# Pooled attention with a top-k MoE layer: long loads and stores, chunk order, dense layers cut into sixteen pieces

## The chip, the cores and the metric

One core of a Trainium2 chip runs the kernel in one launch. The metric is the device time of the launch in microseconds, the median of the runs. TensorE (PE, with its weight loads PEld), VectorE (DVE), ScalarE (ACT), GpSimd (POOL) and SyncE (SP, which here only issues DMAs) each run their own list of instructions in order and wait for one another by semaphores.

## The reference, cut to what matters

```python
# q, k, v: (8 batches, 8 heads, 576 tokens, 64) float32
k_p, v_p = mean over 8 neighbouring tokens        # 72 pooled tokens a head
attn = softmax(q @ k_p.T / 8);  x = attn @ v_p    # -> x: (8, 576, 512)
scores = x @ w_gate                               # one number a token
out = x.copy()
for b in range(8):                                # the 128 best tokens of each batch
    top = argpartition(-scores[b], 128)[:128]
    ye  = relu(x[b, top] @ w1) @ w2               # 512 -> 1024 -> 512
    out[b, top] += sigmoid(scores[b, top])[:, None] * ye
```

## The kernel before, in words

All the work is in `direct_path`; `general_path` runs only if a softmax sum is out of range, which it isn't here. Scheduling is by hand: the order in which the Python code calls its functions is the order on each engine.

A batch has 576 tokens, taken as six **chunks** of 96 (`C`); two chunks are a **unit** (`u`, 24 of them). For each batch the kernel loads K, Q and V, sums K and V over groups of eight tokens (`pool_k`, `pool_v`, three or four GpSimd additions each, L184 to L202), transposes K and Q by DVE (`k_trans` L191, `q_trans` L212), multiplies them (`scores`, L222) and takes the exponential on ACT (L227). `attend` (L237) multiplies a chunk's exponentials with the value sums; two more columns of these give the softmax sum and the gate score. `norm` (L249 to L254, all DVE) reads that result from PSUM, divides, and puts the chunk in `xs`. The PSUM tile `pA` of `attend` has one buffer, so the next `attend` waits for `norm`.

Then follows the MoE layer of the batch, while later batches attend: `store_x` writes `xs` to the output, `score` sums the gate scores, `row_bcast` spreads them over partitions, `count` (L315 to L319, six of them) ranks each token, `one_hot` and `gather` find the 128 best rows and fetch them from the output by an indirect DMA that GpSimd issues (L341), `x_trans` (L353) transposes them on TensorE, `hidden` (L369) and `finish` (L380) are the two dense layers, and a second indirect DMA (L386) writes the rows back.

The main loop goes over units and has five slots in each. A table, `jobs`, filled by `at(u, slot, ...)`, says in which slot of which unit a step of the MoE layer stands. `hidden` and `finish` stand there in four pieces each, for one batch all within two units of the three of a batch. All loads and stores are issued by SP, in the order of the code; a load waits there until its buffer is free. K goes in by four DMAs of 24 or 32 partitions, a Q of a batch by three of 128 partitions, V by two halves of 64 and 8 partitions; `store_x` writes six DMAs of 16 partitions.

Of the kernel before, what the change touches and what calls it, by code (L numbers as in the profile page):

```python
# [830 lines left out]
```

## Time and profile before

| | us |
|---|---|
| median of three runs | 385.44 (384.58 to 387.45) |
| profiled execution, its own time | 386.28 |
| its span, first to last instruction | 384.7 |
| PE busy | 289.5 (75%) |
| PEld busy | 226.8 (59%) |
| DVE busy | 173.1 (45%) |
| POOL busy | 153.4 (40%) |
| ACT busy | 57.4 (15%) |

The profile is of one execution. "Busy" is time in which an engine executed something; matmuls are pipelined and their ends modelled, so PE's busy time is not work at full speed. The granted clock is the share of TensorE's 2.4 GHz that the chip allowed: 1.0 is 2.4 GHz, 0.5 is 1.2 GHz. Times in the trace are counted from the start of the span.

### The profile page before, as it was taken

What the parts mean: (1) busy time and instruction counts of PE and PEld (TensorE: products, weight loads), DVE (VectorE), ACT (ScalarE), POOL (GpSimd) and SP (SyncE); (2) the same over time, 40 slices, a digit from 0 to 9 for tenths busy, and PEclk for the clock granted to TensorE, in tenths of its full rate; (3) what the DMA queues carried; (4) which work ended last, traced back from release to release, by engine and by line L of the source; (5) the groups of instructions that cost most, each with busy time, mean ns of one, the idle gap of its engine ahead of it and who ended that gap; (6) DMA issues with size and microseconds to landing.
All of it is one profiled execution on the core that took longest, in us unless ns stands there. A gap on an engine that the chain in (4) does not pass through costs nothing.

```text
span 384.7 us, 5966 instructions
## 1 busy us (share of the span) xinstructions
PE 289.5 (75%) x2306; PEld 226.8 (59%) x2306; DVE 173.1 (45%) x664; ACT 57.4 (15%) x73; POOL 153.4 (40%) x165
## 2 busy tenths in 40 slices
PE   0228888534999589959996899768994999896890
PEld 0127776432885378539863787457853985782750
DVE  2503535924366433924392528452574338346000
ACT  1001112100221112101220122021210131010100
POOL 0277911465612782068506670478017500202001
PEclk9999856555999688975998599967997699789697
DMA  8999999989798469715993389436000420160001
GB/s 179 254 187 231 347 200 156 180 177 200 157 173 158 95 137 170 145 27 118 196 160 77 89 178 179 104 89 125 2 0 27 103 51 0 56 123 28 29 0 37
DMA packets 18041, 47.55 MB, mean 124 GB/s; under 512 B 2252, under 2 KB 2252, under 8 KB 17172
## 3 DMA queue, kind: packets, MB, share of 16 engines
q1 hardware_dynamic: 16724, 42.88, 55.1%
q0 software_dynamic: 1280, 4.20, 3.5%
q8 instruction: 20, 0.33, 0.4%
q14 instruction: 17, 0.14, 0.1%
HBM read 35.54 MB, written 11.53 MB: 122 GB/s over the span
## 4 chain that ended last, share of the span: by engine, by line
DMA 30%; issue 20%; POOL 19%; PE 14%; SPq 11%; DVE 4%; ACT 0%; POOLq 0%; ACTq 0%
DMA vraw<-in_v_dram 11%; DMA kraw<-in_k_dram 7%; DMA qraw<-in_q_dram 7%; SPq L100 5%; PE pM L369 5%; POOL vraw L198 5%; DMA xr<-out_dram,idx 5%; SPq L275 4%; PE pF L380 3%; POOL kraw L184 3%; POOL vraw L199 3%; PE pA L237 3%; PE pS L222 2%; POOL vp L200 2%; POOL vraw L202 1%
## 5 line engine op out<-in xcount | busy, mean ns | idle before, releaser
L237 PEld LDWEIGHTS pA<-vp,et 72*96 72x96 f32 x768 | 86.4, 195 | 31.8 <-issue 25.4
L237 PE MATMUL pA<-vp,et 72*96 72x66 f32 x768 | 89.8, 280 | 18.4 <-DVE vp L203 10.2
L222 PE MATMUL pS<-qt,kt 32*72 32x192 f32 x768 | 55.1, 445 | 31.6 <-DVE zin L293 15.8
L369 PE MATMUL pM<-xg,w 128*128 128x128 f32 x512 | 75.3, 311 | 1.4 <-ACT xg L355 0.7
L369 PEld LDWEIGHTS pM<-xg,w 128*128 128x128 f32 x512 | 70.8, 222 | 4.2 <-issue 2.1
L222 PEld LDWEIGHTS pS<-qt,kt 32*72 32x72 f32 x768 | 37.9, 192 | 45.6 <-DVE zin L293 17.7
L380 PE MATMUL pF<-w,ht 128*128 128x512 f32 x128 | 61.2, 607 | 0.0
L227 ACT ACTIVATE et<-pS 72x1536 f32<-72x1536 f32 x24 | 34.7, 1446 | 116.9 <-PE pS L222 116.9
L337 POOL TENSOR_SCALAR idx<-tok 128x1 int32<-128x1 f32 x8 | 2.0, 245 | 124.9 <-DVE g L339 124.9
L249 DVE TENSOR_SCALAR zall<-pA 96x8 f32<-96x8 f32 x48 | 7.4, 155 | 94.0 <-PE pA L237 94.0
L198 POOL TENSOR_TENSOR vraw<-vraw 72x1024 f32<-72x1024 f32 x16 | 37.7, 2356 | 16.9 <-DMA vraw<-in_v_dram 16.8
L252 DVE TENSOR_TENSOR xs<-pA,rz 96x512 f32<-96x512 f32 x48 | 32.9, 686 | 2.1
L380 PEld LDWEIGHTS pF<-w,ht 128*128 128x128 f32 x128 | 22.3, 191 | 19.3 <-issue 19.3
L317 DVE TENSOR_SCALAR_CACHE_REDUCE cmp<-sr,sc 96x576 bf16<-96x576 f32 (+5 forms) x48 | 26.6, 554 | 6.1 <-ACT sr L305 6.1
L184 POOL TENSOR_TENSOR kraw<-kraw 128x1536 f32<-128x1536 f32 x7 | 24.0, 3430 | 12.0 <-DMA kraw<-in_k_dram 12.0
L203 DVE TENSOR_REDUCE vp<-vraw 72x4 f32<-72x256 f32 x16 | 6.6, 416 | 46.8 <-POOL vraw L202 46.8
L353 PE MATMUL pM<-ident,xr 128*128 128x128 f32 x32 | 7.6, 381 | 23.5 <-DMA xr<-out_dram,idx 23.5
L212 DVE STREAM_TRANSPOSE qt<-qraw 128x768 f32<-128x768 f32 x24 | 23.0, 963 | 0.0
L386 POOL DMA_INDIRECT out_dram<-y,idx x8 | 8.5, 1064 | 35.2 <-DVE seen L471 20.1
L372 ACT ACTIVATE ht<-pM 128x512 f32<-128x512 f32 x16 | 9.6, 597 | 86.6 <-PE pM L369 86.6
L315 DVE TENSOR_SCALAR_CACHE_REDUCE cmp<-sr,sc 96x96 bf16<-96x96 f32 (+4 forms) x40 | 20.3, 506 | 1.2
L199 POOL TENSOR_TENSOR vraw<-vraw 72x512 f32<-72x512 f32 x16 | 20.3, 1266 | 1.3
(63 smaller groups left out, 194.3 us busy)
## 6 DMA issues: line engine op xcount, KB each, us to landing
qraw<-in_q_dram SPq DMA_DIRECT2D x24, 384.0 KB
out_dram<-xs SPq DMA_DIRECT2D x48, 192.0 KB
vraw<-in_v_dram SPq DMA_DIRECT2D x16, 512.0 KB
kraw<-in_k_dram SPq DMA_DIRECT2D x24, 288.0 KB
w<-in_moe_w_dram SPq DMA_DIRECT2D x2, 2048.0 KB
kraw<-in_k_dram SPq DMA_DIRECT2D x8, 384.0 KB
vraw<-in_v_dram SPq DMA_DIRECT2D x16, 64.0 KB
wg<-in_moe_w_gate_dram SPq DMA_DIRECT2D x1, 144.0 KB
```

Source lines behind the costliest of these rows:

```text
L184: eng.tensor_tensor(out=x[:, :, 0:4, :], in0=x[:, :, 0:4, :], in1=x[:, :, 4:8, :], op=OP.add)
L198: eng.tensor_tensor(out=x[:, :, 0:4, :], in0=x[:, :, 0:4, :], in1=x[:, :, 4:8, :], op=OP.add)
L199: eng.tensor_tensor(out=x[:, :, 0:2, :], in0=x[:, :, 0:2, :], in1=x[:, :, 2:4, :], op=OP.add)
L212: nc.vector.transpose(out=QT[u].rearrange("p j t c -> p t j c"), in_=QR[u].rearrange("p t (j e) -> p t j e", j=2))
L222: nc.tensor.matmul(p[:, i, N3 * s : N3 * s + N3], KT[b][r, j, KG * s : KG * s + KG, :].rearrange("p g r -> p (g r)"), QT[u][r, j, :, G * s ...
L227: nc.scalar.activation(ET[u].rearrange("p (i s) n -> p i (s n)", s=2), p[:, :, 0 : 2 * N3], AF.Exp, scale=exp_scale)
L237: nc.tensor.matmul(p[:, g, E * a : E * a + E], ET[u][:, h, C * cc : C * cc + C], VP[b][:, h, :], start=True, stop=True)
L252: nc.vector.tensor_tensor(out=XS[b][:, c, :].rearrange("p (g a d) -> p g a d", g=2, d=D), in0=o[:, :, :, 0:D], in1=rz.to_broadcast([C, 2, ...
L315: nc.vector.tensor_scalar(cmp[:, 0 : c * C], row[:, 0 : c * C], s, None, op0=OP.is_ge, op1=OP.add, accum_out=CN[b][:, c, 0:1])
L317: nc.vector.tensor_scalar(cmp[:, c * C : S], row[:, c * C : S], s, None, op0=OP.is_gt, op1=OP.add, accum_out=CN[b][:, c, 1:2])
L369: nc.tensor.matmul(p[:, NQ * (f4 % 2) + f, :], w1[:, d, 128 * fc : 128 * fc + 128], XG[b][:, d, :], start=(d == 0), stop=(d == DB - 1))
L380: nc.tensor.matmul(p, HT[b][:, f, :], w2[:, f, :], start=(f == 0), stop=(f == FB - 1))
```

## The change

Loads: K and Q of a batch are one DMA each over 128 partitions, 9 KB to a partition; the first V and the gate weights are issued by ACT. A partition of K now holds four and a half groups of tokens, so GpSimd sums quads only, DVE transposes the half sums (128 x 576 instead of 128 x 384) and adds them in pairs. Tokens are dealt to chunks otherwise (token 6p + c is row p of chunk c), so that a unit's store is one DMA of 96 partitions with 4 KB runs, issued by ACT; ACT writes the exponentials in permuted order for it. In `norm` ACT does the addition to the softmax sum and copies the gate column; the gate product is taken once a batch. `one_hot` is one DVE instruction instead of six. The range check of the sums is done once, at the end.

Order: the loop goes over chunks (`a`, 48 of them). `hidden` and `finish` are cut into eight pieces each and dealt over six chunks, two or three in a chunk. GpSimd's K sums, V sums and the gather have places of their own, and `k_trans` no longer stands behind a V sum. `row_bcast` uses the PSUM tile `pM` instead of `pF`.

```diff
     def load_k(b):
-        x = KRAW[b % 2].rearrange("p r t d -> p (r t d)")
-        run = KR * POOLW * D
-        for i in range(4):
-            n = 32 if b < 2 else 2 * KG
-            nc.sync.dma_start(
-                out=x[32 * i : 32 * i + n, :],
-                in_=bass.AP(tensor=k.tensor, offset=k.offset + (b * H + 2 * i) * S * D, ap=[[run, n], [1, run]]),
-            )
+        KR[b] = work.tile([128, TG, D], FT, name="kraw")
+        nc.sync.dma_start(out=KR[b], in_=k[b].rearrange("h (g t) d -> (h g) t d", g=G))
...
     def pool_k(b, eng):
-        x = KRAW[b % 2]
-        KS[b] = work.tile([128, KR, D], FT, name="ks", bufs=1)
-        eng.tensor_tensor(out=x[:, :, 0:4, :], in0=x[:, :, 0:4, :], in1=x[:, :, 4:8, :], op=OP.add)
+        x = KR[b].rearrange("p (r t) d -> p r t d", r=R)
+        KS[b] = work.tile([128, R, D], FT, name="ks", bufs=1)
         eng.tensor_tensor(out=x[:, :, 0:2, :], in0=x[:, :, 0:2, :], in1=x[:, :, 2:4, :], op=OP.add)
         eng.tensor_tensor(out=KS[b], in0=x[:, :, 0, :], in1=x[:, :, 1, :], op=OP.add)
...
+        nc.vector.tensor_tensor(out=KT[b].rearrange("p j s n -> p (j s n)"), in0=x[:, :, 0], in1=x[:, :, 1],
+                                op=OP.add)
...
-        nc.vector.tensor_scalar(z, o[:, :, :, D], 1e-9 * POOLW, None, op0=OP.add)
...
+        nc.scalar.activation(z.rearrange("p (g n) -> p g n", g=2), o[:, :, :, D], AF.Identity, bias=eps)
+        nc.scalar.copy(out=SS[b][:, c, :].rearrange("p (g n) -> p g n", g=2), in_=o[:, :, :, D + 1])
...
-    def store_x(b):
-        dst = out[b].rearrange("(g c t) d -> t g c d", g=G, c=NC)
-        store[b] = []
-        for t in range(CT):
-            i = nc.sync.dma_start(out=dst[t], in_=XS[b][G * t : G * t + G, :, :])
...
+    def store_x(u):
+        b, th = divmod(u, NTH)
+        c = slice(2 * th, 2 * th + 2)
+        i = nc.scalar.dma_start(out=out[b].rearrange("(p c) d -> p c d", c=NC)[:, c, :], in_=XS[b][:, c, :])
...
+    for u in range(NU):
+        at(2 * u + 2, 1, store_x, u)
     for b in range(B):
...
+        e = NC * (b + 1)
+        last = b == B - 1
+        at(e - 1, 3, score, b)
+        at(e, 2, row_bcast, b, 0)
+        at(e, 3, row_bcast, b, 1)
+        for c in range(NC):
+            at(e + (1 if last else (2, 2, 3, 3, 4, 5)[c]), 3, count, b, c)
+        at(e + (2 if last else 5), 3, one_hot, b)
+        at(e + (5 if last else 6), 3 if last else 1, gather, b)
+        at(e + 7, 1, gate, b)
+        at(e + 7, 3, x_trans, b)
+        for n, f in enumerate((0, 1, 2, 3, 4, 5, 8, 6, 7, 9, 10, 11, 12, 13, 14, 15)):
+            c = (0, 0, 1, 1, 2, 2, 2, 3, 3, 3, 4, 4, 4, 5, 5, 5)[n]
+            slot = (1, 2, 1, 2, 1, 2, 2, 1, 2, 2, 1, 2, 2, 1, 2, 2)[n]
+            at(e + 8 + c, slot, *((hidden, b, f) if f < 8 else (finish, b, f - 8)))
+        if b + 1 < B:
+            a = NC * b
+            at(a, 0, pool_k, b + 1, nc.gpsimd)
+            at(a + 1, 3, pool_v, b + 1, 0, nc.gpsimd)
+            at(a + 2, 1, k_trans, b + 1)
+            at(a + 3, 3, pool_v, b + 1, 1, nc.gpsimd)
+            at(a + 4, 3, gate_v, b + 1, 0)
+            at(a + 5, 3, gate_v, b + 1, 1)
```

What this moves on GpSimd, one batch's turn in the middle of the program. Before, from the K sums (L184 to L186) over the gather (L337 its indices, L341 the DMA) to the first V sums and the scatter (L386):

```order
L184 TENSOR_TENSOR kraw_70<-kraw_70 128x6x256
L185 TENSOR_TENSOR kraw_70<-kraw_70 128x6x128
L186 TENSOR_TENSOR ks<-kraw_70 128x384
L337 TENSOR_SCALAR idx<-tok 128x1
L341 DMA xr<-out_dram,idx 128x512
L346 TENSOR_SCALAR g<-g 128x1
L198 TENSOR_TENSOR vraw<-vraw 72x4x256
L199 TENSOR_TENSOR vraw<-vraw 72x4x128
L200 TENSOR_TENSOR vp_121<-vraw 72x4x64
L202 TENSOR_TENSOR vraw<-vp_121,wg 72x4x64
L386 DMA out_dram<-y,idx 4608x512
```

Now, the same turn:

```order
L169 TENSOR_TENSOR kraw<-kraw 128x9x128
L170 TENSOR_TENSOR ks<-kraw 128x576
L327 TENSOR_SCALAR idx<-tok 128x1
L331 DMA xr<-out_dram,idx 128x512
L340 TENSOR_SCALAR g<-g 128x1
L374 DMA out_dram<-y,idx 4608x512
L186 TENSOR_TENSOR vraw<-vraw 72x4x256
L187 TENSOR_TENSOR vraw<-vraw 72x4x128
L188 TENSOR_TENSOR vp_92<-vraw 72x4x64
L190 TENSOR_TENSOR vraw<-vp_92,wg 72x4x64
```

Both pairs of V sums now follow the scatter, and K's sums are two instructions instead of three. On DVE, before, the stretch from the one-hot rows to the next batch's transposed K (L191); L203 sums the gate column of V, L293 and L294 are the range check:

```order
L327 TENSOR_SCALAR oh<-slots,rank 96x128 x6
L335 TENSOR_REDUCE tok<-pM 128x1
L339 TENSOR_REDUCE g<-pM 128x1
L347 RECIPROCAL g<-g 128x1
L203 TENSOR_REDUCE vp_123<-vraw 72x4
L191 STREAM_TRANSPOSE kt<-ks 128x6x64
```

Now K is transposed (L175) and added in pairs (L179) two chunks into a batch, ahead of two counts (L301 to L309), and the V column (L194) comes later. The rows are from the first batches, where the steps of the batch before stand beside them:

```order
L247 RECIPROCAL rz<-zall 96x8
L248 TENSOR_TENSOR xs<-pA,rz 96x512
L175 STREAM_TRANSPOSE kh<-ks 128x9x64
L179 TENSOR_TENSOR kt<-kh 128x288
L204 STREAM_TRANSPOSE qt<-qraw 128x6x4x32
L301 MEMSET cn 96x1
L307 TENSOR_SCALAR cmp,cn<-sr,sc 96x576
L309 SCALAR_TENSOR_TENSOR cmp,cn<-sr,sc,before 96x96
L305 TENSOR_SCALAR cmp,cn<-sr,sc 96x96
```

The V column no longer stands between a batch's gather and its K. On TensorE, before, from the last piece of a batch's second layer (L380) to the next batch's dense work:

```order
L380 MATMUL pF<-w_131,ht 128x512 x2
L237 MATMUL pA<-vp_121,et 96x66 x8
L353 MATMUL pM<-ident,xr 128x128 x4
L222 MATMUL pS<-qt,kt 72x192 x16
L237 MATMUL pA<-vp_121,et 96x66 x8
L369 MATMUL pM<-xg,w_130 128x128 x8
L237 MATMUL pA<-vp_123,et 96x66 x8
L369 MATMUL pM<-xg,w_130 128x128 x8
```

Now (L216 scores, L368 second layer, L293 `row_bcast`, L232 `attend`, L346 transposed rows, L358 first layer):

```order
L216 MATMUL pS<-qt,kt 72x2x96 x16
L368 MATMUL pF<-w_104,ht 128x512 x2
L293 MATMUL pM<-ident,sc 96x96 x6
L232 MATMUL pA<-vp_94,et 96x66 x8
L368 MATMUL pF<-w_104,ht 128x512 x3
L346 MATMUL pM<-ident,xr 128x128 x4
L232 MATMUL pA<-vp_94,et 96x66 x8
L358 MATMUL pM<-xg,w_103 128x128 x4
L216 MATMUL pS<-qt,kt 72x2x96 x16
L358 MATMUL pM<-xg,w_103 128x128 x4
L232 MATMUL pA<-vp_94,et 96x66 x8
L358 MATMUL pM<-xg,w_103 128x128 x8
```

Between the gather's product and the transposed rows there are now a score group, `row_bcast`, an attend and five pieces of the second layer; before there was one piece and one attend.

## Rows read from the trace of the kernel before

**Rows 1.** Three stretches: busy us (instructions) by engine, granted clock, DMA share, GB/s.

```profile
0.00:95.90 95.90, 50.33 (x416) 41.14 (x416) 41.63 (x131) 11.54 (x11) 45.89 (x46) 0.75 0.97 211
95.90:334.40 238.50, 203.46 (x1717) 159.42 (x1714) 119.28 (x476) 41.99 (x54) 102.90 (x109) 0.86 0.53 106
334.40:384.70 50.30, 35.76 (x179) 26.19 (x178) 12.16 (x57) 3.85 (x8) 4.62 (x10) 0.84 0.18 41
```

**Rows 2.** Waits of PE in 95.9 to 334.4: total us, times, longest.

```profile
PE pS L222 <- DVE zin L293: 15.8, 5, 3.6
PE pM L353 <- DMA xr<-out_dram,idx: 10.3, 6, 2.2
```

**Rows 3.** Timeline, 206 to 216 us: start, length, engine, line, group [idle before, releaser].

```profile
206.59 2.36 POOL L198 TENSOR_TENSOR vraw<-vraw 72x1024 f32<-72x1024 f32 x1
211.87 0.42 DVE L203 TENSOR_REDUCE vp<-vraw 72x4 f32<-72x256 f32 x1 [5.02 <-POOL vraw L202]
212.21 0.84 DVE L191 STREAM_TRANSPOSE kt<-ks 128x384 f32<-128x384 f32 x1
213.11 2.85 PE L222 MATMUL pS<-qt,kt 32*72 32x192 f32 x32 [3.12 <-DVE zin L293]
215.88 2.83 PE L237 MATMUL pA<-vp,et 72*96 72x66 f32 x16
```

**Rows 4.** The two stretches around it: granted clock third from last.

```profile
182.00:206.00 24.00, 22.76 (x205) 16.92 (x203) 14.56 (x62) 4.97 (x7) 7.21 (x6) 1.00 0.88 166
213.00:222.00 9.00, 8.89 (x64) 7.98 (x65) 4.51 (x16) 1.45 (x1) 6.70 (x8) 0.50 0.47 105
```

**Rows 5.** Timeline, PE at the higher clock.

```profile
186.23 1.54 PE L222 MATMUL pS<-qt,kt 32*72 32x192 f32 x32
190.91 2.00 PE L369 MATMUL pM<-xg,w 128*128 128x128 f32 x16
192.75 1.50 PE L237 MATMUL pA<-vp,et 72*96 72x66 f32 x16
200.57 1.93 PE L380 MATMUL pF<-w,ht 128*128 128x512 f32 x4
```

**Rows 6.** Timeline, PE in the first batches.

```profile
22.93 1.52 PE L237 MATMUL pA<-vp,et 72*96 72x66 f32 x8 [4.29 <-DVE vp L203]
29.50 2.85 PE L222 MATMUL pS<-qt,kt 32*72 32x192 f32 x32
39.21 2.70 PE L222 MATMUL pS<-qt,kt 32*72 32x192 f32 x32
```

**Rows 7.** Groups by line and shape: busy us, mean ns, idle before.

```profile
L249 DVE TENSOR_SCALAR zall<-pA 96x8 f32<-96x8 f32 x48 | 7.4, 155 | 94.0 <-PE pA L237 94.0
L251 DVE RECIPROCAL rz<-zall 96x8 f32<-96x8 f32 x48 | 9.6, 199 | 1.7
L252 DVE TENSOR_TENSOR xs<-pA,rz 96x512 f32<-96x512 f32 x48 | 32.9, 686 | 2.1
L345 ACT ACTIVATE g<-g 128x1 f32<-128x1 f32 x8 | 1.6, 203 | 45.5 <-DVE g L339 45.5
L317 DVE TENSOR_SCALAR_CACHE_REDUCE cmp<-sr,sc 96x576 bf16<-96x576 f32 x8 | 6.4, 805 | 6.1 <-ACT sr L305 6.1
L184 POOL TENSOR_TENSOR kraw<-kraw 128x1536 f32<-128x1536 f32 x7 | 24.0, 3430 | 12.0 <-DMA kraw<-in_k_dram 12.0
```

**Rows 8.** Line 319: lengths in ns, shortest, median, longest.

```profile
L319 DVE SCALAR_TENSOR_TENSOR cmp<-sr,sc,before x48: 307/310/2586, 65.3 to 348.9; 96x96 bf16<-96x96 f32 x48
```

**Rows 9.** Timeline: its longest, and GpSimd beside it.

```profile
65.61 3.42 POOL L184 TENSOR_TENSOR kraw<-kraw 128x1536 f32<-128x1536 f32 x1 [9.71 <-DMA kraw<-in_k_dram]
66.56 2.59 DVE L319 SCALAR_TENSOR_TENSOR cmp<-sr,sc,before 96x96 bf16<-96x96 f32 x1
```

**Rows 10.** Stretch in which the dense weights arrive.

```profile
40.00:48.00 8.00, 6.63 (x69) 5.63 (x65) 4.15 (x12) 1.45 (x1) 7.55 (x7) 0.81 1.01 382
```

**Rows 11.** DMA issues: the gather, us from issue to landing.

```profile
xr<-out_dram,idx POOLq DMA_INDIRECT x8, 3.5
```

More of the change, by code (lines that the diff above doesn't have):

```diff
@@ L322, in one_hot @@
     def one_hot(b):
-        rank = work.tile([C, NC], FT, name="rank")
-        nc.vector.tensor_reduce(out=rank, in_=CN[b], axis=AX.X, op=OP.add)
+        rank = work.tile([C, NC, 1], FT, name="rank")
+        nc.vector.tensor_reduce(out=rank[:, :, 0], in_=CN[b], axis=AX.X, op=OP.add)
         OH[b] = work.tile([C, NC, cap], BF, name="oh", bufs=1)
-        for c in range(NC):
-            nc.vector.tensor_scalar(OH[b][:, c, :], slots, rank[:, c : c + 1], None, op0=OP.is_equal)
+        nc.vector.tensor_tensor(out=OH[b], in0=slots.rearrange("p (one n) -> p one n", one=1).to_broadcast([C, NC, cap]),
+                                in1=rank.to_broadcast([C, NC, cap]), op=OP.is_equal)
     def gather(b):
@@ L393, in direct_path, with at @@
     jobs = {}
[L395 to L396 removed]
+    def at(a, slot, *job):
+        jobs.setdefault((a, slot), []).append(job)
+    for u in range(NU):
+        at(2 * u + 2, 1, store_x, u)
     for b in range(B):
[L399 to L421 removed]
@@ L423, in run @@
-    def run(u, slot):
-        for f, *a in jobs.get((u, slot), ()):
-            f(*a)
+        e = NC * (b + 1)
[9 more added lines that the diff above has]
+        at(e + 7, 3, x_trans, b)
@@ L427, in direct_path, with run @@
+        if b + 2 < B:
+            at(a, 1, load_k, b + 2)
+            at(a + 1, 1, load_q, b + 2)
+            at(a + 2, 1, load_v, b + 2, 0, nc.sync)
+            at(a + 4, 3, load_v, b + 2, 1, nc.sync)
+    def run(a, slot):
+        for f, *x in jobs.get((a, slot), ()):
+            f(*x)
     pool_k(0, nc.vector)
+    pool_v(0, 0, nc.gpsimd)
     k_trans(0)
@@ L430, in direct_path @@
     scores(0)
+    pool_v(0, 1, nc.vector)
+    gate_v(0, 1)
+    gate_v(0, 0)
     q_trans(1)
+    load_k(1)
     for g in range(2):
-        pool_v(0, g, nc.gpsimd)
-    load_k(1)
+        load_v(1, g, nc.sync)
     load_q(1)
-    load_v(1)
-    load_weights()
-    for u in range(NU + 6):
-        b, th = divmod(u, NTH)
-        live = u < NU
-        more = b + 1 < B
-        run(u, 0)
-        if live:
-            attend(u, 0)
-            norm(u, 0)
-        run(u, 1)
-        if u + 1 < NU:
-            scores(u + 1)
-        if u + 2 < NU:
-            q_trans(u + 2)
-        run(u, 2)
-        if live:
-            attend(u, 1)
-            norm(u, 1)
-        run(u, 3)
-        if more:
-            if th == 0:
-                pool_k(b + 1, nc.gpsimd)
-            else:
-                pool_v(b + 1, th - 1, nc.gpsimd)
-            if th == 1:
-                k_trans(b + 1)
-        if b + 2 < B:
-            (load_k, load_q, load_v)[th](b + 2)
-        run(u, 4)
+    constants()
+    nc.sync.dma_start(out=w1, in_=moe_w1.rearrange("(a p) f -> p a f", p=128))
+    at(3, 1, lambda: nc.sync.dma_start(out=w2, in_=moe_w2.rearrange("(a p) n -> p a n", p=128)))
+    for a in range(NCH + 14):
+        run(a, 0)
+        if a < NCH:
+            attend(a)
+            norm(a)
+        run(a, 1)
+        u = a // 2
+        if a % 2 == 0 and u + 1 < NU:
+            scores(u + 1)
+            if u + 2 < NU:
+                q_trans(u + 2)
+        run(a, 2)
+        run(a, 3)
+    z = zall.rearrange("p b c h -> p (b c h)")
+    zin = work.tile([C, NCH * H], FT, name="zin", bufs=1)
     seen = const.tile([C, 1], FT)
-    nc.vector.tensor_reduce(out=seen, in_=cnt, axis=AX.X, op=OP.add)
+    nc.vector.tensor_scalar(zin, z, POOLW * ZLO, None, op0=OP.is_ge)
+    nc.vector.scalar_tensor_tensor(zin, z, POOLW * ZHI, zin, op0=OP.is_le, op1=OP.mult, accum_out=seen)
     p = psum.tile([1, 1], FT, name="pM")
     nc.tensor.matmul(p, seen, ones, start=True, stop=True)
-    nc.vector.tensor_scalar(flag, p, float(C * B * NC * H), None, op0=OP.is_lt)
+    nc.vector.tensor_scalar(flag, p, float(C * NCH * H), None, op0=OP.is_lt)
 def general_path(ctx, tc, q, k, v, moe_w_gate, moe_w1, moe_w2, moe_capacity, out):
```

231 lines of the change are left out of this document (100 added, 131 removed).

## The prediction, made before the result

> **What bounds the kernel now.** I cut the span into three stretches first [rows 1]: 95.9 us to the first attend of the third batch, 238.5 us for the attends of the other six batches, 50.3 us of dense work behind the last attend. The reader is to see in the middle one that PE is busy 203.5 of 238.5 us at a granted clock of 0.86, while DMA is at 0.53, DVE at half and POOL below half. So two things are lost there: 35 us in which PE waits, and the clock. At full clock the same work is 203.5 x 0.86 = 175 us, 29.2 a batch, against 238.5 / 6 = 39.8 that a batch takes.
>
> The list of waits says for what PE waits [rows 2]: the next batch's scores, put down to a DVE instruction, up to 3.6 us, and the transposed rows for the gather's DMA, up to 2.2. The timeline shows why [rows 3]: GpSimd takes the first V sum at 206.6, in its list right behind the gather that it waited for, and DVE transposes K behind that V sum at 212.2, so PE begins its scores at 213.1. Then the clock: the scores that take 1.54 us at the higher level take 2.85 here, an attend 2.83 for 1.50 [rows 3, 5]; the stretch behind the wait runs at 0.50 (1.2 GHz) for 9 us, the one ahead of it, in which PE hardly rested, at 1.00 (2.4 GHz) [rows 4]. One such turn in each batch is what separates 39.8 from 29.2.
>
> In the first stretch DMA is at 0.97 with 211 GB/s [rows 1]; the dense weights, loaded over 128 partitions, came at 382 [rows 10]. PE's units of two chunks there follow each other in 9.7 us, from score group to score group, each at the long duration [rows 6].
>
> **The change part by part.** The sum is made against the profiled execution: 386.28 us, of which 384.7 span and 1.6 around it. It is 0.8 above the median of 385.44; I take that off at the end.
>
> *First stretch.* One K load over 128 partitions, V on ACT's queue beside it and half of the first V sums on DVE bring the first attend forward from 22.9 [rows 6]. It waited there for GpSimd's V sums, about 5.5 us from the first addition to the reduced column [rows 3]. Halving them and a quicker load give 17; nothing gained gives 23; I take 20. Six units of 9.7 follow, since attends without dense work between them run at the long duration in these rows and the change puts dense work no earlier: 58. If they ran at the higher level a unit would be two attends, a score group and one wait for `norm`, about 6.2 [rows 5], and 37. One `row_bcast` adds 1. Sum 79 for 95.9, bounds 58 and 83. The loads are off this path as long as 16 MB (three batches, weights, a store) come in 79 us, which is the rate of now.
>
> *The wait for K and the low clock behind it.* K's sums are 1152 + 576 elements; at 3.43 us for 1536 [rows 7] that is 3.9 us, and they and the transposition come five chunks ahead of the scores that use them. This wait goes: up to 3.6 a batch. The gather's wait goes too, if GpSimd issues it in time: behind five small casts and 3.9 us of K sums, the DMA is issued some 6 us after the chunk begins and lands 3.5 later [rows 11]; between product and transposition PE now has a score group, five pieces of the second layer, `row_bcast` and an attend, about 9 us. That is even; I cost it at nothing, and at 2 a batch as the upper bound, when loads are in flight beside it.
>
> *Smaller pieces.* Sixteen pieces of half a step (a first-layer piece is half of 2.00, a second-layer one half of 1.93 [rows 5]) in more switches: 0.5 a batch. The wait of `row_bcast` for ACT stays as it is, 0.7.
>
> *ACT in `norm`.* Addition and reciprocal were 155 and 199 ns on DVE, the division 686 [rows 7]; the small ACT row took 203. One more handover and about 0.1 us longer: behind every attend two pieces or a score group follow, at least 1.9 us, against a chain of some 1.6. So it is hidden, but only where DVE is on time. The Trainium skill (ScalarE: Activation LUTs, Rules for kernel authors) would leave additions on VectorE, and prices a small ACTIVATE with a per-partition bias at about 0.28 us; by that the sum would be at most 6 us longer (0.13 for each of 48 chunks), if all were exposed.
>
> *What is late next.* DVE. The pinch is in the third and fourth chunk of a batch, where K's transposition and two counts a chunk stand. Between the end of the third chunk's attend and the attend of the fifth, PE has four first-layer pieces, a score group and an attend: 7.0 us. DVE has two norms (0.9 each), K's transposition (576 for 384 elements: 0.84 [rows 3] becomes 1.2), the pair addition (0.4), a Q transposition (about 1.0), two counts (0.805 [rows 7] + 0.31 [rows 8] + 0.1 = 1.2 each) and two handovers of 0.25: 7.3. On top of that comes GpSimd. A two-operand DVE instruction that met a GpSimd addition took 2.59 us for 0.31 and ended with it [rows 8, 9]; before, this happened hardly ever, because GpSimd stood waiting for the gather while the counts ran. Now both V sums are beside the counts, and three DVE instructions in the pinch have two operands (the pair addition and L309 twice): each waits between 0 and 2.36 [rows 3], 0.8 as a mean over GpSimd's four lengths. Bounds of PE's new wait: 0.3 and 7.4; I take 2, nearest to 0.3 + three times 0.8 less what GpSimd's gaps spare.
>
> This is the Trainium skill's lock (SBUF — State Buffer, Who interferes with whom): a DVE instruction with two SBUF inputs and a GpSimd one that reads SBUF exclude each other. The trace agrees [rows 9], with 2.59 for 0.31. By it alone the change moves work to where it collides.
>
> *The clock behind the new wait.* Waits of 1.6 and 3.1 us were followed by 9 us at the lower level [rows 3, 4]. A wait of 2 will often do the same. At 0.86 the middle stretch now has some 11 us of the lower level in each batch, two waits together. I take one fall a batch of about 7 us, at half speed 3.4 us lost; bounds 0 and 6.8 (14 us, a little above what two waits cost now).
>
> *Middle stretch.* A batch: 29.2 + 0.7 + 0.5 + 2.0 + 3.4 = 35.8; six are 214.5, less 6 for dense work that now lies behind the stretch, 208.5 for 238.5.
>
> *Last stretch.* The dense work begins about three chunks later than before, so two whole batches of it stand behind the last attend: 2 x 14.9 us (16 pieces), the remainder of a third 5, two gathers' chains beside it, transposed rows and small waits 9, and some 9.5 from the last product to the end as before: 53.5 for 50.3, bounds 50 and 58. The range check, now 1 us of DVE at the end, lies beside the last scatter.
>
> **Sum**: 79 + 208.5 + 53.5 = 341; with 1.6 around it and 0.8 off, **342 us**. Its own range, from the bounds nearest to it, is 330 to 355.
>
> **The rivals.**
>
> *The clock holds (0.27).* If the V sums and counts miss each other, the wait in the pinch is 0.9 and nothing falls: 6 x 31.3 - 6 = 182 for the middle, and 304 to 326 in all, by whether the first units still run long (79) or not (about 62). For it: the stretch from 182 to 206, with the same mixture of attends and dense pieces, stayed at 1.00 [rows 4]. Against it: PE had no wait above a microsecond in there.
>
> *Two waits a batch (0.17).* The gather comes late as well, and each batch is at 1.2 GHz for 14 us: 29.2 + 0.7 + 0.5 + 3 + 2 + 6.8 = 42.2; 247 for the middle and 355 to 384 in all. For it: the loads now run ahead without stores between them and meet the gather's DMA. Against it: GpSimd is free of V sums when the gather's indices come.
>
> *The loads are no faster (0.04).* The shape does nothing and 211 GB/s stays. V keeps its 64 + 8 partitions. 16 MB then take 79 us with stores and gather beside them perhaps 88: 350.
>
> *Slower (0.06).* With dense pieces of 1 us between attends and a wait in every other chunk, the clock doesn't rise at all in the middle stretch. An all-low batch is 29.2 x 1.88 (2.83 for 1.50) = 55 + 2: 57, and 470 in all. It decides from 7 us more a batch than I forecast: when TensorE is at 1.2 GHz for half of a batch's 43 us instead of a fifth. For it: attends and scores alone never got the short duration in the first units [rows 6]. Against it: dense pieces are half of PE's time from chunk 14 on, the same share as in 182 to 206.
>
> **How the numbers follow.** Forecast 0.46, the others as given. About 1% (4 us) is what a measurement of this kernel can tell from no change. Faster by over 1%: 0.46 + 0.27 + 0.04 and most of the 0.17, 0.90; within 1%: the upper end of two waits, 0.04; slower 0.06. The range leaves out the lower third of the first rival, the upper third of the second, and the slower one: 308 to 372, which takes in the bounds of the first attends (58 to 83) on one side and of the fall (6.8) on the other.
>
> **What would show it.** Right: the first attend near 20 and the seventh unit's near 79; no wait of the scores on K; PE's longest wait in a batch for a DVE `norm`, in the fifth chunk, with L309, L179 or L316 at two to eight times its shortest length beside a GpSimd V sum; one stretch of 0.5 a batch behind it; the last stretch 50 to 58 us. Wrong: units of 6 to 7 us at the start; a middle stretch at 1.00 throughout; PE waiting for the gather's DMA in each batch; ACT's store issues holding up the exponentials, which I cost at nothing since the scores take longer than an issue; DMA above 0.9 behind 95 us.

## The result, and the profile after

The changed kernel takes 366.3 us (median, 365.58 to 367.31) against 385.66 for the kernel before on the same chip: ratio 0.950, 95% interval 0.945 to 0.954. The forecast was 342, range 308 to 372. The direction was right; the gain was 19 us where 43 were expected. Ratios here and below compare undisturbed runs only, so one can differ a little from that of the medians.

The profiled execution has a span of 364.9 us. Cut as [rows 1] is, with the time ahead of the first attend apart (columns as there; the clock record of this trace begins at 38.0 us, and ahead of it the view prints 1.00):

```profile
0.00:32.96 32.96, 2.85 (x33) 1.91 (x33) 14.50 (x13) 4.21 (x2) 14.57 (x18) 1.00 0.60 166
32.96:94.63 61.67, 46.74 (x391) 39.51 (x391) 28.87 (x87) 20.79 (x32) 21.51 (x22) 0.65 0.79 242
94.63:312.65 218.02, 185.94 (x1667) 148.74 (x1668) 119.00 (x364) 74.29 (x122) 91.17 (x103) 0.89 0.40 113
312.65:364.90 52.25, 39.65 (x218) 26.14 (x217) 15.58 (x62) 5.57 (x13) 7.25 (x14) 0.94 0.11 35
```

| stretch | before | forecast | after | after less forecast |
|---|---|---|---|---|
| to the first attend | 22.9 | 20 | 33.0 | +13.0 |
| six units and `row_bcast` | 73.0 | 59 | 61.7 | +2.7 |
| middle | 238.5 | 208.5 | 218.0 | +9.5 |
| last | 50.3 | 53.5 | 52.3 | -1.2 |

So the missed 24 us lie at the start and in the middle. The waits of TensorE in the middle stretch, as [rows 2]:

```profile
PE pA L232 <- DVE xs L248: 12.3, 5, 3.3
PE pM L293 <- ACT sr L295: 8.6, 6, 2.7
PE pA L232 <- DVE vp L194: 6.5, 6, 1.4
PE pM L346 <- DMA xr<-out_dram,idx: 6.2, 4, 3.3
```

The scores' wait for K (15.8 us before) is gone. The first line is the new wait for `norm`, forecast 12 (six of 2): four in the fifth chunk of a batch, 10.8 us together, and one of 1.5 that still belongs to the first units. The second line was forecast 4.2, the other two nothing.

**The start.** The timeline, columns as [rows 3]:

```profile
16.72 2.35 POOL L186 TENSOR_TENSOR vraw<-vraw 72x1024 f32<-72x1024 f32 x1 [15.17 <-DMA vraw<-in_v_dram]
23.14 1.22 DVE L186 TENSOR_TENSOR vraw<-vraw 72x1024 f32<-72x1024 f32 x1 [11.17 <-DMA vraw<-in_v_dram]
24.40 3.62 DVE L187 TENSOR_TENSOR vraw<-vraw 72x512 f32<-72x512 f32 x1
24.86 2.61 POOL L169 TENSOR_TENSOR kraw<-kraw 128x1152 f32<-128x1152 f32 x1
29.59 2.44 DVE L190 TENSOR_TENSOR vraw<-vp,wg 72x256 f32<-72x256 f32 x1
32.96 2.80 PE L232 MATMUL pA<-vp,et 72*96 72x66 f32 x16 [18.09 <-DVE vp L194]
```

V0, now on ACT's queue, lands at 16.7 and 23.1 us. Then DVE's half of the V sums meets GpSimd's sums of the next K and V: L187 takes 3.62 us (0.69 where it stands alone, in h1 below) and L190 2.44 (0.42). The DMA queues from 5 to 13 us, when both have loads waiting (q1 is SP's, q10 ACT's; packets, MB, share of the 16 engines):

```profile
q1 hardware_dynamic: 254, 2.05, 80.5%
q10 hardware_dynamic: 247, 0.51, 20.9%
```

Each queue gets as many packets as the other. SP's are nearly all of 9 KB (a partition of K or Q), ACT's of 2 KB (a partition and head of V), so V0 gets a fifth of the bytes.

**The fifth chunk**, as forecast: K's pair addition and L309, with two operands, stand beside V sums of GpSimd, and TensorE's attend waits 3.27 us for `norm`.

```profile
230.81 2.35 POOL L186 TENSOR_TENSOR vraw<-vraw 72x1024 f32<-72x1024 f32 x1
231.17 2.10 DVE L309 SCALAR_TENSOR_TENSOR cmp<-sr,sc,before 96x96 bf16<-96x96 f32 x1
234.87 0.69 DVE L248 TENSOR_TENSOR xs<-pA,rz 96x512 f32<-96x512 f32 x1
235.61 2.54 PE L232 MATMUL pA<-vp,et 72*96 72x66 f32 x16 [3.27 <-DVE xs L248]
```

The stretches around it, granted clock third from last, as [rows 4]: 2.4 GHz with the wait in it, then 1.2 GHz for 6.5 us, then 2.4 again. The same wait stands in the fifth chunk of three other batches, at 160.4, 198.8 and 272.6 us (3.17, 1.82 and 2.58 us). Behind the first and the last of these the clock falls too, behind the 1.82 it doesn't. The other long stretch at the lower level is the start of the middle one, which comes from the first units:

```profile
228.00:236.00 8.00, 4.73 (x48) 4.54 (x45) 7.76 (x19) 3.66 (x4) 7.61 (x7) 1.00 0.01 3
236.00:242.50 6.50, 6.50 (x54) 5.54 (x53) 5.02 (x20) 0.32 (x2) 0.05 (x1) 0.50 0.21 63
243.00:273.00 30.00, 25.20 (x236) 19.84 (x236) 16.27 (x43) 12.60 (x19) 16.41 (x18) 1.00 0.23 65
94.63:120.00 25.37, 18.01 (x140) 15.30 (x141) 10.39 (x32) 5.83 (x12) 16.67 (x18) 0.57 0.56 164
160.30:168.50 8.20, 8.08 (x64) 6.96 (x65) 5.54 (x23) 1.22 (x3) 0.57 (x1) 0.58 0.24 54
272.50:280.00 7.50, 7.36 (x59) 6.24 (x60) 5.66 (x23) 0.87 (x3) 1.77 (x3) 0.57 0.18 52
```

**ACT**, groups by line as [rows 7]; L227 is the exponential of the kernel before:

```profile
L227 ACT ACTIVATE et<-pS 72x1536 f32<-72x1536 f32 x24 | 34.7, 1446 | 116.9 <-PE pS L222 116.9
L220 ACT ACTIVATE et<-pS 72x1536 f32<-72x1536 f32 x24 | 70.7, 2947 | 61.9 <-PE pS L216 61.9
L244 ACT ACTIVATE zall<-pA,eps 96x8 f32<-96x8 f32 x48 | 12.2, 254 | 93.8 <-PE pA L232 93.8
```

The exponential takes 2.95 us; before, the same size took 1.45. It is the same function on the same elements, written in permuted order, in steps of 24 bytes. ACT is busy 104.9 us (57.4 before).

### The profile page after: what moved, and what is told of

The parts are those of the page before. It is cut to its first block, busy times and chain, and to the rows that moved or that the text cites. A ratio compares the mean times of both kernels' runs of the same rounds, so it can differ in the third digit from the quotient of the medians.

```text
span 364.9 us, 5869 instructions
## 1 busy us (share of the span) xinstructions
PE 275.2 (75%) x2306; PEld 216.3 (59%) x2306; DVE 177.9 (49%) x524; ACT 104.9 (29%) x169; POOL 134.5 (37%) x156
## 4 chain that ended last, share of the span: by engine, by line
PE 44%; DVE 22%; DMA 16%; ACT 6%; issue 5%; POOL 4%; ACTq 1%; DVEq 0%; SPq 0%; POOLq 0%
PE pA L232 14%; PE pM L358 10%; PE pS L216 8%; DMA xr<-out_dram,idx 8%; PE pF L368 8%; DMA vraw<-in_v_dram 7%; DVE xs L248 4%; ACT et L220 4%; DVE cmp L309 3%; POOL kraw L169 2%; DVE cmp L305 2%; DVE qt L204 2%; DVE cmp L307 2%; DVE oh L316 2%; DVE kh L175 2%
## 5 line engine op out<-in xcount | busy, mean ns | idle before, releaser
L232 PE MATMUL pA<-vp,et 72*96 72x66 f32 x768 | 90.8, 281 | 47.7 <-DVE vp L194 24.6
L232 PEld LDWEIGHTS pA<-vp,et 72*96 72x96 f32 x768 | 86.3, 195 | 59.0 <-issue 28.5
L220 ACT ACTIVATE et<-pS 72x1536 f32<-72x1536 f32 x24 | 70.7, 2947 | 61.9 <-PE pS L216 61.9
L358 PE MATMUL pM<-xg,w 128*128 128x128 f32 x512 | 71.3, 292 | 2.8 <-ACT xg L348 1.5
L358 PEld LDWEIGHTS pM<-xg,w 128*128 128x128 f32 x512 | 65.0, 203 | 8.7 <-issue 5.0
L368 PE MATMUL pF<-w,ht 128*128 128x512 f32 x128 | 65.2, 632 | 0.0
L247 DVE RECIPROCAL rz<-zall 96x8 f32<-96x8 f32 x48 | 9.5, 198 | 113.9 <-ACT zall L244 112.4
L216 PE MATMUL pS<-qt,kt 32*72 32x192 f32 x768 | 52.4, 428 | 12.0 <-DVE qt L204 12.0
L216 PEld LDWEIGHTS pS<-qt,kt 32*72 32x72 f32 x768 | 36.5, 184 | 19.4 <-DVE qt L204 12.0
L186 POOL TENSOR_TENSOR vraw<-vraw 72x1024 f32<-72x1024 f32 x15 | 35.5, 2368 | 19.7 <-DMA vraw<-in_v_dram 19.6
L244 ACT ACTIVATE zall<-pA,eps 96x8 f32<-96x8 f32 x48 | 12.2, 254 | 93.8 <-PE pA L232 93.8
L368 PEld LDWEIGHTS pF<-w,ht 128*128 128x128 f32 x128 | 22.9, 200 | 17.9 <-issue 17.9
L309 DVE SCALAR_TENSOR_TENSOR cmp<-sr,sc,before 96x96 bf16<-96x96 f32 x48 | 21.9, 456 | 0.3
L373 DVE SCALAR_TENSOR_TENSOR y<-pF,g,xr 128x512 f32<-128x512 f32 x8 | 6.0, 750 | 29.5 <-PE pF L368 29.5
L187 POOL TENSOR_TENSOR vraw<-vraw 72x512 f32<-72x512 f32 x15 | 19.1, 1277 | 1.2
```

The source lines that it names most:

```text
L186: eng.tensor_tensor(out=x[:, :, 0:4, :], in0=x[:, :, 0:4, :], in1=x[:, :, 4:8, :], op=OP.add)
L187: eng.tensor_tensor(out=x[:, :, 0:2, :], in0=x[:, :, 0:2, :], in1=x[:, :, 2:4, :], op=OP.add)
L216: nc.tensor.matmul(p[:, i, 2 * s : 2 * s + 2, 0:C], KT[b][r, j, s, :], QT[u][r, :, j, :, G * s : G * s + G], start=(j == 0), stop=(j == 1))
L220: nc.scalar.activation(ET[u].rearrange("p n g t -> p n t g"), p.rearrange("p i n x -> p (i n) x")[:, :, 0:C].rearrange("p n (t g) -> p n t ...
L232: nc.tensor.matmul(p[:, g, E * n : E * n + E], ET[u][:, 2 * h + cc].rearrange("p g t -> p (g t)"), VP[b][:, h, :], start=True, stop=True)
L309: nc.vector.scalar_tensor_tensor(cmp[:, 0:C], row[:, c * C : c * C + C], s, before, op0=OP.is_equal, op1=OP.mult, accum_out=CN[b][:, c, 2:3])
```

## The experiments

All are edits of the changed kernel; "less" is against its 366.3 us.

**V0 on SP (h1), and a fourth V buffer (h3).**

```diff
-    load_v(0, 0, nc.scalar)
+    load_v(0, 0, nc.sync)
...
-    load_v(0, 1, nc.scalar)
+    load_v(0, 1, nc.sync)
...
-        x = work.tile([SP, HG, POOLW, D], FT, name="vraw", bufs=3)
+        x = work.tile([SP, HG, POOLW, D], FT, name="vraw", bufs=4)   # h3 alone
```

> The first V loads are issued by SP, in the order K0, V0 first half, Q0, V0 second half, and no longer by ACT; nothing else changes. Theory (V0's 2 KB packets starved beside the 9 KB packets of K0, Q0 and K1): V0 lands near 12 and 15 us, the first attend moves from 32.96 to 20 to 25 us, the seventh unit's from 94.6 to 82 to 87, and the median from 366.3 to 354 to 359. Rival 1 (the bytes themselves take that long, whatever queue): first attend at 29 or later, median 362 or more. Rival 2 (the additions of V that exclude each other on DVE and GpSimd are the whole delay): V0 lands by 15, but the first attend stays at 28 or later.

> As h1_v0_on_sp, and V has four buffers instead of three, so that the second half of batch 1's V no longer waits on SP ahead of Q1, the first dense weights and K2. Theory: SP's hold of some 30 us at the start was only a symptom; DMA is busy between 20 and 33 us, but the seventh unit's attend stands within 1.5 us of h1_v0_on_sp and the median too (354 to 359). Rival (the loads behind the held one are late for the first units): the seventh unit's attend is 3 to 6 us earlier than in h1_v0_on_sp, median 348 to 353.

h1: 356.35 us (ratio to before 0.917, 0.909 to 0.924), 10 less. Timeline:

```profile
18.07 1.22 DVE L186 TENSOR_TENSOR vraw<-vraw 72x1024 f32<-72x1024 f32 x1 [2.84 <-DMA vraw<-in_v_dram]
21.85 2.80 PE L232 MATMUL pA<-vp,et 72*96 72x66 f32 x16 [3.72 <-DVE vp L194]
```

The first attend comes at 21.85. The seventh unit's came at 88.2, later than expected, since the constants on DVE now met GpSimd's sums (k1 below).

h3: 368.63 us (0.951, 0.944 to 0.958), 12 slower than h1, which neither theory had. The first attends agree (22.75), and the middle loses: TensorE's wait for the gathered rows between 90 and 300 us, in h1 and in h3:

```profile
PE pM L346 <- DMA xr<-out_dram,idx: 8.1, 4, 3.1
```

```profile
PE pM L346 <- DMA xr<-out_dram,idx: 19.2, 4, 6.2
```

In h1 SP's V issues take 27.9 us from 95.6 on, since the second half waits for a buffer, and the next K waits behind it. In h3 Q, V and K go out within 4.3 us, around the issue of the gather at 98.2 (SP's queue, h1, then h3):

```profile
95.55 27.86 SPq L106 DMA_DIRECT2D vraw<-in_v_dram  x4
```

```profile
97.11 3.39 SPq L106 DMA_DIRECT2D vraw<-in_v_dram  x4
```

The gather then takes a median of 8.9 us to land in these batches, 7.2 in h1. That the held load had kept the queues clear for it fits these times; no run varied it alone.

**Was it the queue or the packets beside it (h5)?**

```diff
-    load_k(1)
     for g in range(2):
         load_v(1, g, nc.sync)
+    load_k(1)
     load_q(1)
```

> The changed kernel, with the load of K1 on SP behind V1's halves, so that only K0, Q0 and the first half of V1 go out beside V0, which stays on ACT's queue. Theory (V0's 2 KB packets got a small share beside the 9 KB packets): V0's second half lands at 15 to 19 instead of about 23, the first attend at 21 to 27 instead of 33; the median is mixed, since K1 comes later. Rival (ACT's queue is slow by itself, or the bytes decide): V0 lands at 21 or later, first attend 30 or later.

355.85 us (0.919, 0.911 to 0.927). With V0 still on ACT's queue:

```profile
18.97 1.22 DVE L186 TENSOR_TENSOR vraw<-vraw 72x1024 f32<-72x1024 f32 x1 [7.16 <-DMA vraw<-in_v_dram]
23.12 2.80 PE L232 MATMUL pA<-vp,et 72*96 72x66 f32 x16 [8.40 <-DVE vp L194]
```

So the queue is not slow by itself. The first attend comes 9.8 us earlier: 4.2 are the landing (23.1 to 19.0), the rest the sums behind it, which no longer meet GpSimd's K sums (from L186 to the attend 4.2 us instead of 9.8). The Trainium skill (DMA: Bandwidth & Descriptors, Queues, rings and completion order) says that each DMA engine takes turns between queues packet by packet. The trace agrees, with the 254 and 247 packets above. h5 alone would also fit that fewer bytes were in the way; the packet counts show that V0 was held to a fifth of them.

**Constants first (k1)**: h1, and `constants()` called ahead of `pool_k(0, nc.vector)`.

> h1_v0_on_sp, and DVE makes the constants in its idle time before K0 lands instead of behind the first Q transpositions. Theory (in h1_v0_on_sp five of these small instructions met GpSimd's K and V sums, 2.27, 2.11 and 1.31 us for 0.2 each, so the second attend came 9.1 us after the first): that step falls from 9.1 to 5.2 to 6 us, the seventh unit's attend from 88.2 to 84 to 86, the median from 356.4 to 352 to 354. Rival (the first units wait for exponential and GpSimd anyhow): under 1.5 us, 355 to 357.

354.39 us (0.917, 0.913 to 0.921), 2.0 below h1, which the intervals don't tell apart. In the trace the first chunk went from 9.1 to 5.5 us and the seventh unit's attend from 88.2 to 84.5, as expected. For the six first units the clock column and the lengths disagree:

```profile
21.70:84.50 62.80, 51.21 (x390) 43.53 (x391) 26.81 (x70) 20.80 (x32) 28.84 (x25) 1.00 0.78 241
```

```profile
41.22 2.83 PE L232 MATMUL pA<-vp,et 72*96 72x66 f32 x16 [1.42 <-DVE xs L248]
106.44 2.85 PE L216 MATMUL pS<-qt,kt 32*72 32x192 f32 x32
116.28 1.54 PE L216 MATMUL pS<-qt,kt 32*72 32x192 f32 x32
```

That 1.00 is no reading: the clock record of this trace begins at 110.3 us, at 1.00, and the view prints 1.00 where it has no record. The lengths turn there, a score group from 2.85 to 1.54. So these units ran at 1.2 GHz, and last as long as those of the changed kernel. Ahead of a record's start the lengths decide; [rows 1]'s 0.75 for the first stretch counts 41.6 us without a record as 1.00 as well.

**The exponential's permutation, moved to TensorE's reading of Q (e1), to ACT's reading of PSUM (e2), to DVE's transposition of Q (e3).**

```diff
-                QT[u][r, :, j, :, G * s : G * s + G],
+                QT[u][r, :, j, :, G * s : G * s + G].rearrange("p cc t g -> p cc g t"),   # e1
...
-        nc.scalar.activation(ET[u].rearrange("p n g t -> p n t g"),
-            p.rearrange("p i n x -> p (i n) x")[:, :, 0:C].rearrange("p n (t g) -> p n t g", g=G),
+        nc.scalar.activation(ET[u],
+            p.rearrange("p i n x -> p (i n) x")[:, :, 0:C].rearrange("p n (t g) -> p n g t", g=G),   # e2
...
-        QT[u] = work.tile([128, 2, 2, CT, 32], FT, name="qt")
+        QT[u] = work.tile([128, 2, 2, 32, CT], FT, name="qt")   # e3
...
-            out=QT[u].rearrange("p cc j t c -> p t (cc j) c"),
+            out=QT[u].rearrange("p cc j c t -> p t (cc j) c"),   # e3
```

In e1 and e3 the exponential's two patterns are plain.

> TensorE reads Q's columns in the permuted order, so the scores stand in PSUM in the order that attend wants, and the exponential reads and writes plain runs; nothing else changes. Theory: one exponential falls from 2.95 to about 1.45 us, the wait of row_bcast for ACT from 1.19 to about 0.7 and the 2.65 us waits for norm in the first units to about 1.4; median 358 to 363. Rival 1 (the longer exponential lay beside other work): exponential 1.45 and median 365 to 367. Rival 2 (the strided operand slows TensorE): a score group takes 2 us or more at the higher clock instead of 1.54, median 368 or more.

> The exponential reads PSUM in permuted order and writes plain runs; TensorE and DVE as in the changed kernel. Theory (the permuted write to SBUF is what doubles it): exponential about 1.45 us, score group 1.54, row_bcast's wait 0.5; median 358 to 363. Rival (ACT pays for a stride on either side): exponential 2.9, median 365 to 368.

> The permutation is made by DVE's transposition of Q, which writes with a stride of 24 bytes; TensorE and ACT then read and write plain runs. Theory (a 32-bit DVE transposition does not mind where it writes): Q transposition stays near 0.97 us, exponential 1.45, score group 1.54 at the higher clock; median 358 to 363. Rival (a strided write costs DVE as it costs ACT): transposition 1.9 us or more, which makes norm late in the first, third and fifth chunk; median 364 to 370.

e1: 364.67 us (0.942, 0.934 to 0.950), less than 2 us gained. The exponential is 1.45 us, but TensorE pays, as rival 2 had it (not its median of 368): the score group takes 2.83 us where attends around it take 1.50.

```profile
L220 ACT ACTIVATE et<-pS 72x1536 f32<-72x1536 f32 x24 | 34.7, 1447 | 76.9 <-PE pS L216 76.9
```

```profile
198.26 2.83 PE L216 MATMUL pS<-qt,kt 32*72 32x192 f32 x32
```

e2: 356.67 us (0.921, 0.915 to 0.927), 9.6 less. The stride on the side of PSUM costs nothing:

```profile
L220 ACT ACTIVATE et<-pS 72x1536 f32<-72x1536 f32 x24 | 34.7, 1447 | 65.1 <-PE pS L216 65.1
```

e3: 358.30 us (0.921, 0.916 to 0.927). DVE's transposition grows from 0.97 to 1.55 us, between theory and rival:

```profile
L204 DVE STREAM_TRANSPOSE qt<-qraw 128x768 f32<-128x768 f32 x24 | 37.3, 1553 | 0.9 <-DMA qraw<-in_q_dram 0.9
```

So a permuted access to SBUF costs on each of the three engines, and the read from PSUM by ACT doesn't. The Trainium skill (Advanced Engine Details and Errata, SBUF Cachelines) says that an access which meets a new 16-byte line each time is slower. The trace agrees for the 24-byte write: 2.95 for 1.45 us.

**Two counts earlier (c1), and the V column early (c2 = c1 with it).**

```diff
-            at(e + (1 if last else (2, 2, 3, 3, 4, 5)[c]), 3, count, b, c)
+            at(e + (1 if last else (1, 1, 3, 3, 4, 5)[c]), 3 if last else (1, 1, 3, 3, 3, 3)[c], count, b, c)
...
-            at(a + 5, 3, gate_v, b + 1, 1)
+            at(a + 5, 1, gate_v, b + 1, 1)   # c2
```

> The first two counts of a batch move from the third chunk to the second, the other two of the pair behind them stay in the fourth; all else as in the changed kernel. Theory (counts, K's transposition and GpSimd's V sums together make norm late): the wait in the fifth chunk (1.8 to 3.3 us in four batches) goes, and with it the 1.2 GHz stretches behind it; middle stretch 218 to 196 to 206, median 346 to 355. Rival 1 (the low clock does not hang on this wait): only the waits go, middle 206 to 212, median 355 to 361. Rival 2 (the counts now hold up the second layer's last addition, the scatter and so GpSimd): the wait turns up in another chunk, median 363 to 369.

> c1_counts_spread, and the second half of the next batch's V column (L194) stands right behind the norm of the sixth chunk instead of behind the last count, the one-hot rows and the score. Theory (each batch's first attend waits 1.0 us for that column): this wait goes in five batches, median 343 to 346 against 348.8 of c1_counts_spread. Rival (PE gets to its next wait, for the score behind it, that much sooner): 347 to 350.

c1: 348.79 us (0.901, 0.893 to 0.909), 17.5 less. The middle stretch in two parts, and TensorE's waits in it:

```profile
95.10:120.00 24.90, 18.20 (x140) 15.61 (x141) 12.80 (x35) 5.64 (x12) 16.64 (x18) 0.57 0.57 167
120.00:292.80 172.80, 156.48 (x1530) 125.47 (x1530) 103.64 (x329) 68.72 (x111) 74.45 (x85) 0.99 0.42 118
```

```profile
PE pM L293 <- ACT sr L295: 8.7, 6, 2.8
PE pM L346 <- DMA xr<-out_dram,idx: 7.8, 3, 2.6
PE pA L232 <- DVE vp L194: 6.5, 6, 1.4
PE pA L232 <- DVE xs L248: 1.5, 1, 1.5
```

The wait for `norm` falls from 12.3 to 1.5: all four in fifth chunks are gone. The middle stretch falls from 218.0 to 197.7, nearly twice the wait, because the low clock behind it goes too: 0.99 behind 120 us, and 174.7 us of busy time instead of 185.9 for the same work. c2: 343.88 us (0.889, 0.883 to 0.896); the two intervals overlap a little, the 4.9 us are what was expected, and no wait for L194 is left behind the first attend.

**All cures together (b1 = k1, e2 and c2), `norm` back on DVE (d2), Q's load later (l1), TensorE busy beforehand (w1).** The edits against b1 (b1 itself has those of k1, e2 and c2):

```diff
-        nc.scalar.activation(z.rearrange("p (g n) -> p g n", g=2), o[:, :, :, D], AF.Identity, bias=eps)
-        nc.scalar.copy(out=SS[b][:, c, :].rearrange("p (g n) -> p g n", g=2), in_=o[:, :, :, D + 1])
+        nc.vector.tensor_scalar(z..., o[:, :, :, D], 1e-9 * POOLW, None, op0=OP.add)   # d2
+        nc.vector.tensor_copy(SS[b]..., o[:, :, :, D + 1])   # d2
...
-            at(a + 1, 1, load_q, b + 2)
             at(a + 2, 1, load_v, b + 2, 0, nc.sync)
             at(a + 4, 3, load_v, b + 2, 1, nc.sync)
+            at(a + 4, 3, load_q, b + 2)   # l1
...
+    for i in range(30):   # w1, ahead of scores(0)
+        nc.tensor.matmul(warm[:, 0:128], diff, diff, start=True, stop=True)
```

> The cures together: V0 on SP, constants first, the exponential's permutation on its PSUM side, counts spread, the V column early. Theory (each takes away a loss of its own): 343.9 less 11.9 (k1_consts_first) less 9.6 (e2_exp_read_strided), 319 to 326. Rival (the gains overlap, since the exponential's length only counted beside the late norm and the low clock that c1_counts_spread already removes): 328 to 336.

> b1_all_cures, with norm's addition and the copy of the gate column on DVE again, as before the change. Theory (that part of the change is hidden): within 2 us of b1_all_cures. Rival 1 (DVE has no room for 0.3 us more in a chunk): 4 to 10 us slower. Rival 2 (the handover from ACT stands on PE's path wherever attends follow each other closely): 3 to 7 us faster.

> b1_all_cures, with the loads of Q on SP behind both halves of V, so that SP's wait for a V buffer keeps them away from the gather. Theory (the gather's DMA lands late because a Q load of 1.15 MB goes out in its chunk): landing falls from some 7 us to 3.5 to 4.5, TensorE's wait for the gathered rows to under 2 us in all, and the median by 4 to 9 us. Rival (the other loads or the store meet it instead): within 2 us of b1_all_cures.

> b1_all_cures, with 30 products of a constant 128x128 tile, written to an unused PSUM bank, on TensorE before the first scores; they are no part of the result. Theory A (TensorE runs the first units at the long durations because it stood idle for 15 us before): scores and attends of the first units take about 1.5 us, the seventh unit's attend is 10 to 20 us earlier, median 305 to 315. Theory B (the mixture of attends and waits keeps it there, as the prediction took it): the first score group may be short, then 2.8 us again, median within 3 us of b1_all_cures.

b1: 330.98 us (0.857, 0.852 to 0.863), between theory and rival: of the 21.5 us of k1 and e2, 12.9 are left on top of c2. d2: 326.23 (0.844, 0.838 to 0.850), 4.7 faster. That the part on ACT is hidden is refuted. In the first units TensorE's wait for `norm` is 1.30 us instead of 1.41, and the seventh unit's attend comes 1.6 earlier. Over the whole span the waits for `norm` are 2.1 us shorter (8.6 to 6.5) and those for the gathered rows too (15.2 to 13.1), against a new one of 1.3; why the gather's fell was not tested. The Trainium skill (ScalarE: Activation LUTs, Rules for kernel authors) would leave such additions on VectorE, and this run agrees. l1: 324.77 us (0.833, 0.825 to 0.841), faster than b1. In its profile (a run of 326.77 us) the wait for the gathered rows is 11.4 us for 15.2, where the theory had under 2, so by which mechanism it gained is not settled, and m2 shows no more of it. w1: 330.16 (0.857, 0.850 to 0.864), no difference:

```profile
1.10:9.60 8.50, 8.48 (x60) 8.32 (x60) 3.86 (x19) 1.28 (x1) 0.45 (x5) 1.00 0.97 254
15.19 2.85 PE L216 MATMUL pS<-qt,kt 32*72 32x192 f32 x32 [5.56 <-DVE qt L204]
```

The products took 0.14 us each, as L358 does at 2.4 GHz (1.11 for 8), and the score group behind them is long again. But TensorE idled 5.6 us between the two, so theory A is weakened, not refuted.

**The gather ahead of K's sums (m1), and with d2 and l1 (m2).**

```diff
-            at(a, 0, pool_k, b + 1, nc.gpsimd)
+            at(a, 2, pool_k, b + 1, nc.gpsimd)
```

> b1_all_cures, with GpSimd's two K sums behind the gather's index and DMA instead of ahead of them. Theory (the gather is issued some 4 us late, as the prediction priced at nothing): TensorE's wait for the gathered rows falls from 15.2 us in five batches to under 4, the stretches of 0.5 behind it (at 163 and 200 us) go, median 331.0 to 318 to 325. Rival 1 (the gather then meets the same Q and V loads one step earlier, and lands no sooner): wait over 10, median within 2 us of 331. Rival 2 (K's sums come too late for DVE's transposition in the third chunk): the wait moves to norm of the third or fourth chunk, median 329 to 336.

> m1_gather_first, with the loads of Q behind V's (l1_q_load_late) and norm's addition and copy on DVE (d2_norm_on_dve). Theory (the ACT part of norm costs TensorE at the start, where the gather plays no part, and the later loads add little once the gather is early): 4 to 7 us below m1_gather_first, 312 to 320. Rival (both gains were gains of the gather's wait): within 2 us of m1_gather_first.

m1: 317.39 us (0.814, 0.804 to 0.824), 13.6 below b1: the K sums ahead of the gather were the larger part of its lateness. Its wait is 6.2 us, not under 4 as expected, and of b1's two stretches at 0.50 in the middle (from 163.0 and 200.6 us) one is left (from 130.0). m2: 314.04 (0.806, 0.798 to 0.814), not told apart from m1, so neither its theory nor its rival is shown. TensorE's wait for the gathered rows over the whole span, in b1 and in m2:

```profile
PE pM L346 <- DMA xr<-out_dram,idx: 15.2, 5, 4.5
```

```profile
PE pM L346 <- DMA xr<-out_dram,idx: 6.4, 4, 3.1
```

m1 and m2 are the fastest kernels of this study, and both beat the two kernels compared.

**Only the two unforeseen costs removed (f1 = k1 and e2).**

> The changed kernel with only the two costs taken away that the prediction did not have: V0's late landing (V0 on SP, constants first) and the doubled exponential (permutation on its PSUM side). Counts, V column, gather and norm as in the changed kernel. Theory (these two are what separates 366 from the forecast): seventh unit's attend 78 to 82, where the forecast had 79, and a median of 342 to 348. Rival (the middle stretch was mis-sized as well, by the 1.0 us wait for the V column and the gather): 349 to 356.

345.47 us (0.892, 0.885 to 0.899):

```profile
0.00:21.63 21.63, 2.85 (x33) 1.91 (x33) 12.38 (x30) 2.73 (x2) 6.02 (x14) 1.00 0.93 240
21.63:79.80 58.17, 46.60 (x390) 39.53 (x391) 26.81 (x70) 13.02 (x32) 29.09 (x25) 0.59 0.87 255
79.80:289.80 210.00, 181.62 (x1668) 147.21 (x1669) 115.48 (x364) 51.01 (x122) 91.06 (x103) 0.89 0.42 119
289.80:342.20 52.40, 39.60 (x218) 26.12 (x217) 15.57 (x62) 5.57 (x13) 7.25 (x14) 0.94 0.11 35
```

Against the forecast of 20, 59, 208.5 and 53.5 the stretches are 21.6, 58.2, 210.0 and 52.4.

## Why the prediction was wrong, by its own steps

- **The step that failed: "bring the first attend forward from 22.9 ... I take 20".** It came at 33.0, outside the bounds of 17 and 23. "Nothing gained gives 23" was no end: V's move to another queue put its small packets beside larger ones, and half of its sums moved to DVE met GpSimd's sums of the next K and V. The prediction had that collision for the counts [rows 9] and not here. h1, k1 and h5 show both causes; k1 gives back 11.9 us.
- **A cost that had no step: the permuted exponential.** The change was described with it, and the sum gave it nothing. It is 1.5 us longer 24 times; e2 gives back 9.6 us. It also lengthens `row_bcast`'s waits for ACT, 8.6 us in the middle stretch for 4.2 forecast (4.0 in f1). Without these two costs the kernel takes 345.5 (f1), so they are 20.8 of the missed 24.3 us.
- **Right in place, right in sum by luck: the wait in the fifth chunk and the clock behind it.** L309 took 2.10 us beside a V sum, as foreseen. But the wait came in four of the six batches, 2.7 us each, 10.8 in all, where the sum had 2 in every batch, 12. Three of the four were followed by some 7 us at the lower level, 3.3 us lost each as priced: 10 us, not the 20.4 of six falls. At 0.89 the 185.9 us of busy time do hold 20.5 us of lost clock, but 7.7 of them lie ahead of 120 us, where the low clock of the first units goes on, a term that the sum did not have. c1 shows that wait and fall go together: without the four waits the clock behind 120 us is 0.99.
- **Priced at nothing, wrongly: the gather behind K's sums**, 6.2 us here with an upper bound of 12, and **the V column**, 6.5, which had no step. They were partly made up by less busy time, 185.9 us where the forecast's terms without its waits give 192.6. In f1 the middle agrees with the forecast in its sum, not in its parts: there the gather's wait is 14.8 us and `norm`'s 4.5.
- **Called hidden: `norm` on ACT**, by 1.9 us of work against a chain of 1.6. In the first units no dense work follows, and TensorE waits for it. It costs 4.7 us in b1 (d2); what it cost in the changed kernel itself was not run.
- **Right**: units of 9.7 (9.8 measured), the last stretch (52.3 for 53.5), no wait of the scores on K, loads off the path behind 95 us (DMA at 0.40), and ACT's store issues holding up nothing: the exponentials wait for TensorE alone (61.9 us).
- **A sum of the prediction that does not follow from its terms:** the first rival's 304 to 326. Its 182 with 79 or 62, 53.5 and 0.8 give 315 and 298.

## What to carry to other kernels

When a load moves to another queue, ask what shares the DMA engines with it and with which packet size: the result may be later than before, and the range must say so. When an instruction is kept but its access pattern changes, price it anew, and try the permutation on its PSUM side, where it cost nothing here. After curing the longest wait look for the next in the same chunk: here `norm`, then the gather, and each took the clock with it. A sum that agrees can hide terms that don't: compare term by term, and where a clock column and the length of the same instruction disagree, go by the length.

## What the runs showed of the hardware that was not expected

- In steps of 24 bytes in SBUF, ACT's 72x1536 write took 2.95 us for 1.45; ACT's permuted read from PSUM 1.45; TensorE's permuted read of the moving operand 2.83 a score group for 1.54; DVE's permuted 128x768 transposition 1.55 for 0.97.
- Two DMA queues with packets of 9 and 2 KB, both with loads waiting, handed over equal numbers of packets (254 and 247 from 5 to 13 us), so 4 to 1 in bytes.
- One more buffer made the kernel 12 us slower (h3 against h1), with 19.2 us of waiting for the gathered rows instead of 8.1.
